# Converting five of sixteen weight pieces inside the first quads, with x ahead of weights in the queue and the last copies ahead of conversions

## The chip, the cores and the metric

One core of a Trainium2 chip. The time is the device time of one execution in microseconds; each kernel was run beside the kernel it is compared with, on the same chip. Fewer microseconds are better.

## The reference, cut to what matters

```python
Y = np.fft.rfft(x, axis=1) * (filt_r + 1j * filt_i)[None]   # x: 8 images, 3008 x 256
x = np.fft.irfft(Y, n=3008, axis=1).astype(np.float32).reshape(24064, 256)
h = x @ w_in                                # w_in: 256 x 2048, float64
g = np.where(h > 0, h, np.exp(np.minimum(h, 0)) - 1)
out = (g @ w_out).astype(np.float32)        # w_out: 2048 x 256, float64
```

The two weights are float64, and the kernel computes in fp32. So the kernel fetches them as pairs of 32-bit words and builds fp32 numbers out of the bits, once, before or beside the first use. That conversion is what the change moves.

## The kernel before

The work of an image is a chain: x is brought in and transformed (`a_first`, `t_first`), multiplied by the filter (`b_unit`, the "products" on VectorE), transformed back (`bi_unit`), written to DRAM as `yd`, read back in another order, and finished by the matmuls `psn` in `n_unit`. Then come "quads": one quad takes one block of positions and a quarter of the hidden width through both weights, each as seven products of a Strassen scheme. TensorE does `phs`, `pha`, `phd` (first weight) and `po` (second weight) in a quad, and ScalarE and VectorE do the copies, the exponential and the combinations between them. There are 192 quads; only the first four to five matter here, because each meets its quarter of the weights for the first time.

A weight piece is 128 x 512 numbers (0.52 MB); there are sixteen, four for each quarter. This is the conversion of one:

```python
def w_split(k):                       # VectorE: mantissa bits and exponent bits
    nc.vector.tensor_scalar(out=m, in0=hi, scalar1=0x000FFFFF, op0=ALU.bitwise_and, ...)
    nc.vector.tensor_scalar(out=e, in0=hi, scalar1=0x7FF00000, op0=ALU.bitwise_and, ...)
def w_float(k):                       # ScalarE: four ACTIVATEs
    nc.scalar.activation(out=l, in_=wds[k][:, :, 0], func=AXT.Identity, scale=2.0 ** -52)
    nc.scalar.activation(out=f, in_=m, func=AXT.Identity, scale=2.0 ** -20, bias=1.0)
    nc.scalar.activation(out=ef, in_=e, func=AXT.Relu, scale=-8.0, bias=edges[:, 0:1])
    nc.scalar.activation(out=e, in_=ef, func=AXT.Relu, scale=-1.0, bias=edges[:, 1:2])
def w_join(k):                        # VectorE: sign, sum, product; for odd pieces four sums
    ...                               # (cut)
    if j % 2 == 1:
        nc.vector.tensor_tensor(out=s1, in0=a21, in1=a22, op=ALU.add)
        ...                           # three more (cut)
```

The order of the program before, with cuts marked. Each engine gets its own instructions in this order:

```python
TICKS = {0: 8, 1: 9, 3: 10, 5: 11, 7: 12, 8: 13, 9: 14}   # step g: piece k
for c in range(NXC):
    x_load_first(c)
    if 0 < c < 5:
        w_fetch(c, nc.sync)           # weights between the pieces of x
...
for c in range(NXC):                  # pieces 0 to 5 while x is transformed
    w_split(c); w_float(c); a_first(c)
    if c > 0:
        w_join(c - 1); w_fetch(c + 4, ...)
nc.sync.dma_start(gs, gs_d)           # the table of the inverse transform
...                                   # pieces 6 and 7 (cut)
for g in range(NG + 2):               # products, inverse transform, yd
    k = TICKS.get(g)
    if k: w_split(k)
    ...                               # bi_unit(g-2), b_unit(g), y_write(g-2), y_read (cut)
    if k: tick(k)                     # w_float(k), w_join(k-1)
w_split(15); tick(15)
w_join(15)
n_unit(0, 0)                          # psn, and after it the quads
```

And the place in a quad at which TensorE waits. `phs` is one accumulation bank; ScalarE copies it out (`keep`) before TensorE may add the next product to it:

```python
def s1(): keep("t1", mm(1, "s", True))                       # phs <- y
def s2(): add("b11", mm(2, "a", True), g["t1"]); done("a")   # pha <- y
def s6(): keep("t2", mm(6, "s", False))                      # phs <- ys: needs the copy of s1
```

## Time and profile before

The median is 2667.32 us (2666.79 to 2667.9, 4 runs). TensorE is busy for 98% of it, so I follow a few marks on TensorE's timeline: where it starts the last x matmuls and the first transpose, where it starts `psn`, where it starts quad 4 (the first matmul with 256 columns), and where it starts a later `psn` that lies well behind everything the change touches.

| mark (us) | before |
|---|---|
| last x matmuls / first transpose | 46.28 / 52.12 |
| first `psn` | 118.17 |
| quad 4 starts | 168.12, that is 49.95 after `psn` |
| later `psn` | 194.85 |

Two rows of TensorE's timeline carry the last two marks of the table. The columns are the start, the busy time, the engine, the line, the operation with output and inputs, and the shapes:

```profile
168.12 1.03 PE L408 MATMUL phs<-y,wi 128*128 128x256 f32 x4
194.85 1.95 PE L360 MATMUL psn<-tn,t 128*128 128x128 f32 x16
```

### The profile page before, as it was taken

Reading aid. Unit: us, or ns where it says so; the run is one execution under the profiler, and the core shown is the slowest. Engines: PE = TensorE matmul, PEld = TensorE weight load, DVE = VectorE, ACT = ScalarE, POOL = GpSimd, SP = SyncE. Lnnn points to the kernel's source line nnn. Section 1 sums busy time; section 2 is a strip of 40 time slices with the busy share of each in tenths; the row PEclk is TensorE's granted clock in tenths of the full one; section 3 lists DMA queues with packets and bytes.
Section 4 is the critical chain, followed back from the end, with each engine's and each line's share of the span. In section 5 each row is a group of like instructions: output and inputs, shape, how many; then the busy total and the mean of one; then the engine's idle time right before and its main releaser. Section 6 shows DMA issues by size and latency. Waiting matters only on the chain.

```text
span 2665.7 us, 37335 instructions
## 1 busy us (share of the span) xinstructions
PE 2601.9 (98%) x13508; PEld 2213.2 (83%) x13508; DVE 1843.9 (69%) x3203; ACT 1507.8 (57%) x2622; POOL 235.6 (9%) x295
## 2 busy tenths in 40 slices
PE   4799999999999999999999999999999999999998
PEld 3388889888898878988889878898789888899887
DVE  4876767767676776767766776676767677666766
ACT  5555555555555555555555555555555555555554
POOL 4000200012000120002100021000210012000000
PEclk7799999999999999999999999999999999999999
DMA  9533411343124231333314242133421233110010
GB/s 277 129 94 92 109 44 38 92 107 94 38 51 123 77 86 38 86 97 80 78 41 102 73 99 74 38 85 96 105 56 38 68 87 87 39 40 19 21 28 17
DMA packets 224712, 202.85 MB, mean 76 GB/s; under 512 B 127586, under 2 KB 191090, under 8 KB 224528
## 3 DMA queue, kind: packets, MB, share of 16 engines
q1 hardware_dynamic: 212064, 167.23, 25.1%
q0 software_dynamic: 11008, 32.52, 4.7%
q8 instruction: 107, 1.75, 0.3%
q10 hardware_dynamic: 1456, 0.72, 0.1%
q14 instruction: 77, 0.63, 0.1%
HBM read 128.52 MB, written 74.97 MB: 76 GB/s over the span
## 4 chain that ended last, share of the span: by engine, by line
PE 95%; DMA 2%; DVE 1%; issue 0%; ACT 0%; SPq 0%; DVEq 0%; ACTq 0%
PE po L490 43%; PE phs L408 25%; PE phd L408 12%; PE pha L408 6%; PE psn L360 3%; PE pva L297 2%; PE psr L297 2%; PE psa L209 2%; DMA f<-in_moe_w_in_dram 1%; DMA xc<-in_x_dram 1%; PE pvb L297 1%; DMA wd<-in_moe_w_out_dram 0%; PE psi L297 0%; PE po L269 0%; DMA t<-yd 0%
## 5 line engine op out<-in xcount | busy, mean ns | idle before, releaser
L490 PE MATMUL po<-g,wo 128*128 128x256 f32 (+1 forms) x5376 | 1296.7, 375 | 0.0
L490 PEld LDWEIGHTS po<-g,wo 128*128 128x128 f32 x5376 | 1015.0, 190 | 129.5 <-issue 16.2
L419 ACT ACTIVATE g<-phs 128x512 f32<-128x512 f32 (+1 forms) x576 | 338.9, 588 | 844.2 <-PE phs L408 843.6
L416 DVE TENSOR_TENSOR g<-phd,g 128x512 f32<-128x512 f32 (+1 forms) x384 | 259.6, 676 | 463.7 <-ACT e L426 278.0
L426 ACT ACTIVATE e<-e 128x512 f32<-128x512 f32 (+1 forms) x768 | 477.3, 621 | 24.4
L408 PE MATMUL phs<-y,wi 128*128 128x256 f32 (+1 forms) x1536 | 395.1, 380 | 0.0
L408 PE MATMUL phs<-ys,wi 128*128 128x256 f32 (+1 forms) x1536 | 387.6, 375 | 2.5 <-ACT g L419 1.5
L430 DVE SCALAR_TENSOR_TENSOR g<-e,g 128x512 f32<-128x512 f32 (+1 forms) x576 | 387.1, 672 | 0.2 <-ACT e L426 0.2
L425 ACT ACTIVATE e<-g 128x512 f32<-128x512 f32 (+1 forms) x576 | 352.9, 613 | 35.4 <-DVE g L416 29.3
L408 PEld LDWEIGHTS phs<-y,wi 128*128 128x128 f32 x1536 | 284.9, 190 | 83.2 <-ACT t L329 34.1
L408 PEld LDWEIGHTS phs<-ys,wi 128*128 128x128 f32 x1536 | 291.4, 190 | 36.4 <-ACT g L419 2.2
L430 DVE SCALAR_TENSOR_TENSOR g<-e,phs 128x512 f32<-128x512 f32 (+1 forms) x192 | 130.0, 677 | 139.2 <-ACT e L426 139.2
L408 PE MATMUL phd<-ys,wi 128*128 128x256 f32 (+1 forms) x768 | 193.9, 375 | 1.8 <-DVE g L416 1.8
L408 PE MATMUL pha<-y,wi 128*128 128x256 f32 (+1 forms) x768 | 193.7, 375 | 0.0
L408 PE MATMUL phd<-y,wi 128*128 128x256 f32 (+1 forms) x768 | 193.7, 375 | 0.0
L425 ACT ACTIVATE e<-phs 128x512 f32<-128x512 f32 (+1 forms) x192 | 112.9, 588 | 141.4 <-PE phs L408 140.6
L318 POOL TENSOR_TENSOR sr<-sr,sp 128x512 f32<-128x512 f32 x56 | 71.1, 1270 | 1256.2 <-DVE sp L311 1256.2
L408 PEld LDWEIGHTS phd<-ys,wi 128*128 128x128 f32 x768 | 145.7, 190 | 18.9 <-DVE g L416 2.5
L408 PEld LDWEIGHTS pha<-y,wi 128*128 128x128 f32 x768 | 145.8, 190 | 16.5
L408 PEld LDWEIGHTS phd<-y,wi 128*128 128x128 f32 x768 | 145.8, 190 | 16.5
L467 DVE TENSOR_TENSOR g<-g,g 128x512 f32<-128x512 f32 (+1 forms) x192 | 130.7, 681 | 6.6
L470 DVE TENSOR_TENSOR g<-g,g 128x512 f32<-128x512 f32 (+1 forms) x192 | 130.7, 681 | 6.7
(134 smaller groups left out, 2393.1 us busy)
## 6 DMA issues: line engine op xcount, KB each, us to landing
yd<-t SPq DMA_DIRECT2D x127, 192.0 KB
t<-yd SPq DMA_DIRECT2D x190, 128.0 KB
z<-t SPq DMA_DIRECT2D x84, 256.0 KB
f<-fd POOLq DMA_DIRECT2D x112, 192.0 KB, 3.6
t<-z SPq DMA_DIRECT2D x224, 96.0 KB
out_dram<-o SPq DMA_DIRECT2D x632, 32.0 KB
tn<-tn_t SPq DMA_DIRECT2D x48, 256.0 KB
xc<-in_x_dram SPq DMA_DIRECT2D x84, 128.0 KB
```

The source lines that it names most:

```text
L297: nc.tensor.matmul(ps[:, u:u + w, :], table[k, v, :], r[k, u:u + w, :], start=n == 0, stop=n == len(rhs) - 1)
L318: nc.gpsimd.tensor_tensor(out=sr, in0=sr, in1=p, op=ALU.add)
L360: nc.tensor.matmul(ps[:, ts(q, P)], t[:, i - 4 * m, ds(dh * P, P)], w[:, i - 4 * m, :], start=True, stop=True)
L408: nc.tensor.matmul(ps[:, a, 0:h], w_in[q][:, COMBO[n], a, :], y[n], start=start and a == 0, stop=True, skip_group_check=True)
L416: nc.vector.tensor_tensor(out=g[o], in0=i0, in1=i1, op=ALU.add)
L419: nc.scalar.activation(out=g[o], in_=i0, func=AXT.Copy)
L425: nc.scalar.activation(out=e, in_=src, func=AXT.Relu, scale=-1.0)
L426: nc.scalar.activation(out=e, in_=e, func=AXT.Exp, scale=-1.0)
L430: nc.vector.scalar_tensor_tensor(out=g[n], in0=es[n], scalar=1.0, in1=src, op0=ALU.subtract, op1=ALU.max)
L467: nc.vector.tensor_tensor(out=b12, in0=b22, in1=b12, op=ALU.subtract)
L470: nc.vector.tensor_tensor(out=g["t4"], in0=g["b21"], in1=g["t2"], op=ALU.subtract)
L490: nc.tensor.matmul(po[i][:, u, 0:h], w_out[q][:, COMBO[n], a, :], g[n][:, a, :], start=q == 0 and a == 0 and n in (1, 3, 6, 4), stop=True, ...
```

## The change

The intent is to shorten what lies ahead of `psn`. Fewer weight pieces stand in the queue ahead of x; fewer are converted while VectorE does the filter's products; no conversion stands on ScalarE between the last product and the last two copies; and pieces 11 to 15, which the first quads do not need at once, are converted inside those quads. The core of the diff (the choice of buffers for the pieces is cut):

```diff
-        m, e, c = wtmp[k % 2]
+        m, e, c = wtmp[k % 2 if k < 10 else 0]
...
-        if j % 2 == 1:
+        if j % 2 == 1 and k < 11:
+            w_sums(k)                      # the four sums, now a function
...
-        TICKS = {0: 8, 1: 9, 3: 10, 5: 11, 7: 12, 8: 13, 9: 14}
+        TICKS = {0: 4, 1: 5, 3: 6, 4: 7, 6: 8}
...
-                if 0 < c < 5:
-                    w_fetch(c, nc.sync)
+                if c in (1, 3):
+                    w_fetch((c + 1) // 2, nc.sync)
...
-                w_split(c)
-                w_float(c)
+                if c % 2 == 0:
+                    w_split(c // 2)
+                    w_float(c // 2)
                 a_first(c)
-                if c > 0:
-                    w_join(c - 1)
-                    w_fetch(c + 4, nc.sync if c < 4 else nc.gpsimd)
+                if c in (2, 4):
+                    w_join(c // 2 - 1)
+                for k in ((), (3,), (4, 5), (6,), (7,), ())[c]:
+                    w_fetch(k, nc.sync)
             nc.sync.dma_start(gs, gs_d)
...
-            w_split(15)
-            tick(15)
-        w_join(15)
+            for k in (9, 10):
+                w_split(k)
+                tick(k)
+                w_fetch(k + 4)
+        w_join(10)
...
         n_unit(0, 0)
+        w_split(11)
+        w_float(11)
...
+        for (quad, place), steps in {
+            (0, 0): ((w_join, 11),),
+            (0, 1): ((w_sums, 11), (w_split, 12), (w_float, 12)),
+            (1, 0): ((w_join, 12), (w_fetch, 15), (w_split, 13), (w_float, 13)),
+            (1, 1): ((w_join, 13),),
+            (2, 0): ((w_sums, 13), (w_split, 14), (w_float, 14)),
+            (2, 1): ((w_join, 14), (w_split, 15), (w_float, 15)),
+            (3, 0): ((w_join, 15),),
+            (3, 1): ((w_sums, 15),),
+        }.items():
```

Place 0 of a quad is its middle, place 1 its end.

More of the change, by code (lines that the diff above doesn't have):

```diff
@@ L547, in w_fetch @@
         q, j = divmod(k, 4)
-        if k in (3, 4):
-            wd = t2p.tile([P, 4, D], FP32, tag="t2", name="wd").rearrange("p u d -> p (u d)")
-        elif k in (10, 11):
+        if k in (10, 11):
             wd = t1p.tile([P, XC, D], FP32, tag="t1", name="wd").rearrange("p u d -> p (u d)")
-        elif k in (6, 7, 8, 9, 15):
+        elif k in (3, 4, 6, 7):
             wd = xp.tile([P, 2, 2, D], FP32, tag="xc", name="wd").rearrange("p k u d -> p (k u d)")
         else:
-            wd = fbufs[{5: 0, 12: 1, 13: 2, 14: 0}.get(k, k)].rearrange("p c u d -> p (c u d)")
+            wd = fbufs[{0: 0, 5: 0, 12: 0, 15: 0, 1: 1, 8: 1, 13: 1}.get(k, 2)].rearrange("p c u d -> p (c u d)")
         wd = wds[k] = wd.bitcast(U32).rearrange("p (a w) -> p a w", w=2)
@@ L606, in w_join, with w_sums @@
                 nc.vector.tensor_tensor(out=dst[:, i], in0=f[:, i], in1=e[:, i], op=ALU.mult)
-        if j % 2 == 1:
-            w = (w_in if j < 2 else w_out)[q]
-            a11, a21, a12, a22, s1, s2, s4 = (w[:, i] for i in range(7))
-            nc.vector.tensor_tensor(out=s1, in0=a21, in1=a22, op=ALU.add)
-            nc.vector.tensor_tensor(out=s2, in0=s1, in1=a11, op=ALU.subtract)
-            nc.vector.tensor_tensor(out=s4, in0=a12, in1=s2, op=ALU.subtract)
-            nc.vector.tensor_tensor(out=a21, in0=a11, in1=a21, op=ALU.subtract)
+        if j % 2 == 1 and k < 11:
+            w_sums(k)
+    def w_sums(k):
+        q, j = divmod(k, 4)
+        w = (w_in if j < 2 else w_out)[q]
+        a11, a21, a12, a22, s1, s2, s4 = (w[:, i] for i in range(7))
+        nc.vector.tensor_tensor(out=s1, in0=a21, in1=a22, op=ALU.add)
+        nc.vector.tensor_tensor(out=s2, in0=s1, in1=a11, op=ALU.subtract)
+        nc.vector.tensor_tensor(out=s4, in0=a12, in1=s2, op=ALU.subtract)
+        nc.vector.tensor_tensor(out=a21, in0=a11, in1=a21, op=ALU.subtract)
     def f_arrange():
@@ L679 @@
                 f_read(0, g, ff[:, g])
-                if g % 2:
-                    w_fetch(NXC + 4 + g // 2)
+                if 3 <= g < 6:
+                    w_fetch((8, 10, 11)[g - 3])
             for g in range(4):
                 t_first(g)
-            for k in (NXC, NXC + 1):
-                w_split(k)
-                tick(k)
-                w_fetch(k + 8)
+            w_split(3)
+            tick(3)
+            w_fetch(9)
             tn_read(0, 0)
@@ L704 @@
                     tick(k)
-            w_split(15)
-            tick(15)
-        w_join(15)
+                    if k == 6:
+                        w_fetch(12)
+            for k in (9, 10):
[3 more added lines that the diff above has]
+        w_join(10)
         for c in range(2):
@@ L722, in at @@
             plan.setdefault((quad, place), []).append((fn, a))
+        for (quad, place), steps in {
[8 more added lines that the diff above has]
+        }.items():
+            for fn, k in steps:
+                at(quad, place, fn, k)
         for c in range(2, XBUFS):
```

## The prediction

> **What bounds the kernel now.** I read the page first, then busy time by stretch, the chain of waits of the first 135 us, the timeline of each engine there, and last the DMA queues in growing windows.
>
> ```profile
> span 2665.7 us, 37335 instructions
> PE 2601.9 (98%) x13508; PEld 2213.2 (83%) x13508; DVE 1843.9 (69%) x3203; ACT 1507.8 (57%) x2622; POOL 235.6 (9%) x295
> ...
> 0.00:100.00 100.00, 61.40 (x329) 38.50 (x332) 59.23 (x116) 55.26 (x101) 33.58 (x65) 0.73 0.80 220
> ...
> 110.00:120.00 10.00, 1.83 (x8) 1.86 (x9) 7.12 (x16) 5.44 (x10) 0.00 (x0) 0.50 0.70 172
> ...
> 140.00:150.00 10.00, 10.00 (x64) 9.72 (x66) 8.26 (x16) 5.49 (x11) 0.00 (x0) 1.00 0.33 85
> ```
>
> In the two stretch rows PE is the first busy figure, PEclk third from the end. Steady state is TensorE at 98%: nothing that the change touches. Only the preparation (to 118.17 us, first matmul psn) and the first four "quads" (to 169 us) can move. Within them:
>
> ```profile
> 46.28 3.76 PE L250 MATMUL psa<-t,x 128*128 128x128 f32 x16 [7.44 <-DMA x<-in_x_dram]
> 64.21 1.08 PE L297 MATMUL pva<-sr,gs 48*64 48x256 f32 x2 [5.02 <-issue]
> 107.53 0.63 ACT L583 ACTIVATE wfl<-wm 128x512 f32<-128x512 uint32 x1 [2.16 <-DVE wm L576]
> 109.43 0.58 ACT L329 ACTIVATE t<-pva 128x512 f32<-128x512 f32 x1
> 110.52 2.98 DMA yd<-t
> 114.06 3.91 DMA t<-yd
> 118.17 3.75 PE L360 MATMUL psn<-tn,t 128*128 128x128 f32 x16 [12.62 <-DMA t<-yd]
> ```
>
> Three limits follow each other: DMA until x's last piece (46.28); VectorE from 55.16 on, where b_unit products and weight conversions queue behind each other without a gap; at the end ScalarE, whose copy at 109.43 stands behind a conversion that itself waited for VectorE, and then write plus read of yd, 7.6 us, untouched by the change. In the quads ScalarE and VectorE have spare time, but TensorE already waits at one place, the second accumulation into phs, until ScalarE has copied phs out:
>
> ```profile
> 133.06 1.02 PE L408 MATMUL phs<-ys,wi 128*128 128x224 f32 x4 [0.90 <-ACT g L419]
> 59.15 0.42 DVE L613 TENSOR_TENSOR wi<-wi 128x256 f32<-128x256 f32 x1
> 60.16 0.68 DVE L593 SCALAR_TENSOR_TENSOR we<-wd,we 128x512 uint32<-128x512 uint32 x1
> 58.19 0.78 ACT L586 ACTIVATE we<-we,edges 128x512 f32<-128x512 uint32 x1
> q1 hardware_dynamic: 3900, 7.85, 61.9%
> q1 hardware_dynamic: 4705, 9.31, 60.4%
> ```
>
> The last two rows are the SyncE queue's MB by 46 and by 56 us.
>
> **What the Trainium skill says.** "ScalarE: Activation LUTs", What ACT_TABLE_LOAD costs: an ACTIVATE takes 186 ns + 0.833 per element with immediates, 93 more with a pointer bias, and neighbours overlap by about 93. For 512 that is 612 and 706 ns; the trace has 0.61 to 0.69 and 0.70 to 0.78, so it agrees. "VectorE: DVE Perf Modes", the TRN2 errata section: (N+151)/0.96, 691 ns for a 512-wide fp32 tensor_tensor; the trace has 0.68 to 0.69. "DMA: Bandwidth & Descriptors", Queues, rings and completion order: completion is not FIFO per issuing engine. The trace agrees: x's last piece has 7.3 MB up to and with it in its queue, and landed when 7.85 MB had moved. "TensorE: Matmul & The Clock Gate", Part 1: after an idle window of about 3.4 us the array runs at half clock until it has been busy for about as long. The trace agrees: PEclk 0.50 in 110 to 120, and psn's 16 matmuls take 3.75 us at 118 against 1.95 at 142.
>
> **The change part by part.** One piece costs (start to start in the timeline) VectorE 0.68 for the split, 2.0 for the join, 1.6 more for the sums of every second piece; ScalarE 2.54 (57.10 to 59.64) for its four ACTIVATEs.
>
> (1) x ahead of weights. Until x's last piece the queue now carries three 0.52 MB weight pieces, not five: about 6.3 MB. Allowing the same 0.5 MB of skew, that is 6.8 MB moved, which was reached near 36 us. So the last x matmuls start near 37, not 46.3; and the copies out of them no longer stand behind piece 5's conversion, which landed only at 49.1. The transposes can begin near 42.5 (before 52.1), the first product on VectorE near 48 (before 62.83); it must also wait for piece 4, 8.0 MB with skew.
>
> (2) But the table gs, needed by the first bi_unit, stays behind the same eight weight pieces: 9.2 MB, near 56 us whatever the order. VectorE will have finished products 0 and 1 and joins up to piece 4 at about 59. So bi_unit 0 starts near 56 (before 64.21), at half clock again, takes 7 us as before, and product 2 starts near 66.3 instead of 74.23: 7.9 us gained.
>
> (3) From product 2 to product 7 VectorE has six products of 2.4, three joins, two sums and three splits: 25.7 us of work; with the TensorE hand-overs I put product 7 at 93 (before 100.96, also 26.7 us after product 2). Then no conversion stands between product 7 and the copies: 2.4 product, 2.1 matmul, 1.2 copies give 98.7, against 110.5 (9.5 us after product 7's start). Another 3.9 gained. psn would start near 106 instead of 118.17: **12 us gained**. Pieces 9 and 10 are converted under the yd round trip, exactly where 14 and 15 were before.
>
> (4) The five late pieces add 5 x 2.54 = 12.7 us to ScalarE and 5 x 2.7 + 3 x 1.6 = 18 us to VectorE, in four quads of about 11.7 us each, in which VectorE is busy about 32 of 46 us. It could nearly fit, were it spread; but queues are in order. In the changed instruction order, pieces 11, 12 and 15 have their ScalarE part in front of the copy of phs that TensorE waits for, and that part waits for a split which stands on VectorE behind the previous quad's last subtraction and, for 12 and 15, behind sums or a join. Times after psn's start, before against after:
> - quad 0: combine and split 11 end near 7.0, conversion 8.7, copy 9.2; TensorE goes on at 9.25 instead of 6.49: 2.8 lost.
> - quad 1: last subtraction 16.6 + 2.8 = 19.3; sums 20.9; split 21.7; conversion (three ACTIVATEs after the split's first half) 23.3; copy 23.8; TensorE at 23.85 instead of 14.89: 9.0 in all, 6.2 more.
> - quad 2: piece 14's split stands behind piece 13's sums, in front of the x sums and the phd addition: about 2 more.
> - quad 3: join 14 and split 15 (2.7) behind the last subtraction, conversion, copy: TensorE at 58.2 instead of 40.4: 6.7 more.
> - quad 4: sums 15 just before use, about 1 more.
> Sum 18.7. The two idle spells of some 7 us bring half clock for about 4 us each, as after 118: up to 4 us more, of which I count 1.5, since the other engines' lags shrink meanwhile. **20 us lost.** TensorE, at 98% afterwards, cannot win it back.
>
> Sum: 2667.5 - 12 + 20 = 2675.5; I shade it to **2674**, since a loss hung on two-engine waits overlaps more often than my addition allows.
>
> **The rivals.** (a) The deferred work hides: VectorE idles 3.5 us before its phd addition in these quads, and ScalarE is busy about 55%. Then only the preparation counts: 2656, or 2650 if gs comes earlier than I think, for VectorE would be ready for product 2 at 60. For it: the totals nearly fit. Against: the order of instructions, and the 0.90 us wait at 133.06, which shows that there is no slack at that copy. (b) The preparation hardly gains: all bytes must still pass, DMA is saturated to 62 us, and gs might slip to 60 because the filter pieces come through POOL's queue sooner. Then the gain is 8 and the time 2680. For it: DMA share above 1.0 to 60 us. Against: the conversions really leave VectorE's busiest stretch. (c) Late weights stall TensorE: pieces 13 and 14 are fetched only when their buffers are free, near psn, and 15 in quad 1. Landing took 6 to 10 us, and they are used 20 us later; I expect nothing, at worst 2685.
>
> **Range and chances.** All cases lie between 2650 and 2690. I give (a) about a quarter of the weight, my sum with its errors nearly all the rest: 2657 to 2686 should hold it 8 times in 10. Two per cent is 53 us; even the preparation without any idle time, or twice the loss, stays inside. Within 2%: 0.98; 0.01 for each side.
>
> **What would show it.** Step 1: last x matmuls near 37 and transposes near 42.5. Step 2: the first pva matmul near 56, waiting for a DMA. Step 3: last pvb copy near 99 and psn near 106, no conversion on ScalarE between. Step 4: TensorE waits on the ScalarE copy of phs of about 3, 7 and 7 us in quads 0, 1 and 3, PEclk below 1 after the latter two; the busy time per stretch equal to before from quad 5 on. It is wrong if quad 4 starts less than 8 us after its old distance of 50 us from psn, or if psn starts before 100 or after 112.

## More of the kernel before

From TensorE's waits between 97 and 215 us (total, times, longest):

```profile
PE psn L360 <- DMA t<-yd: 12.6, 1, 12.6
PE phs L408 <- ACT g L419: 1.5, 2, 0.9
```

The reader sees one long wait, for the trip of `yd` through DRAM, and almost none at the copy of `phs`.

## The result and the profile after

The changed kernel is correct and takes 2681.78 us (median of 4 runs, 2679.35 to 2682.55), against 2667.32 beside it. The ratio is 1.0053 with a 95% interval of 1.0035 to 1.0070: within 2%, but a real loss of about 14 us. Ratios here are the mean time of one kernel's fast runs over the mean of the other's in the same rounds, so they are not quite the ratio of the medians that I quote.

| mark (us) | before | after | difference |
|---|---|---|---|
| last x matmuls end | 50.04 | 40.44 | -9.6 |
| first transpose | 52.12 | 40.28 | -11.8 |
| first product on VectorE | 62.83 | 45.67 | -17.2 |
| first inverse matmul (`pva`) | 64.21 | 56.76 | -7.5 |
| last copy ahead of `yd` ends | 110.5 | 100.1 | -10.4 |
| `psn` | 118.17 | 107.86 | -10.3 |
| quad 4, distance from `psn` | 49.95 | 72.81 | +22.9 |
| later `psn` | 194.85 | 208.44 | +13.6 |

The preparation gained 10.3 us and the first quads lost 23.9 (22.9 by the start of quad 4 and 1.0 inside it). At the last `psn` of the run, 2558.73 before and 2572.32 after, the difference is still 13.59: nothing later moved.

TensorE's timeline in the preparation of the changed kernel shows what still held it:

```profile
33.87 6.57 PE L250 MATMUL psa<-t,x 128*128 128x128 f32 x32 [5.86 <-DMA t<-tf_t]
56.76 1.08 PE L297 MATMUL pva<-sr,gs 48*64 48x256 f32 x2 [9.28 <-DMA gs<-gs_t]
```

In brackets are the idle time before the row and what ended it. x was done early, as intended. After the transposes and the first matmuls on them TensorE stood for 9.28 us until the table `gs` landed, which is behind eight weight pieces in the queue.

TensorE's waits between 97 and 215 us, the same list as before:

```profile
PE phs L408 <- ACT g L419: 17.7, 4, 7.0
PE psn L360 <- ACT wfl L581: 8.9, 1, 8.9
PE po L490 <- DVE wo L614: 0.8, 1, 0.8
```

The wait on the copy of `phs` has grown from 1.5 to 17.7 us. The second line is a wait on the `yd` read that the list puts down to the last thing that ended before it; the ScalarE row that it names has nothing to do with `psn` (in experiments 1 and 3 the list puts the same wait down to `DMA t<-yd`).

The timeline of TensorE in quads 0 to 4 shows the three long waits at this place and what follows them:

```profile
116.83 1.02 PE L408 MATMUL phs<-ys,wi 128*128 128x224 f32 x4 [3.63 <-ACT g L419]
118.49 1.86 PE L408 MATMUL phs<-ys,wi 128*128 128x224 f32 x4 [0.63 <-ACT g L419]
...
132.82 1.86 PE L408 MATMUL phs<-ys,wi 128*128 128x224 f32 x4 [6.96 <-ACT g L419]
134.47 3.19 PE L490 MATMUL po<-g,wo 128*128 128x224 f32 x8
...
169.33 1.86 PE L408 MATMUL phs<-ys,wi 128*128 128x224 f32 x4 [6.49 <-ACT g L419]
170.98 2.57 PE L490 MATMUL po<-g,wo 128*128 128x224 f32 x8
...
180.67 1.03 PE L408 MATMUL phs<-y,wi 128*128 128x256 f32 x4
```

Look at the durations: four `phs` matmuls take 1.86 us after the two longest waits, and after the first wait from the second group on, where they take 1.02 at full clock; eight `po` matmuls take 3.19 and 2.57 instead of 1.68. The stretches of the same time say why (after the stretch and its length, the first figure is the time in which PE was busy; PEclk, the granted TensorE clock with 1.00 for full, is the third from the end):

```profile
118.00:122.00 4.00, 3.51 (x11) 3.24 (x12) 2.80 (x7) 2.02 (x4) 0.00 (x0) 0.57 1.08 199
132.00:139.00 7.00, 6.18 (x20) 5.25 (x24) 4.48 (x8) 1.31 (x3) 1.24 (x2) 0.53 0.24 77
169.00:173.00 4.00, 3.67 (x10) 3.37 (x11) 3.62 (x7) 0.82 (x2) 0.00 (x0) 0.53 0.00 0
```

TensorE is busy, at about half its clock, three times. Why the copy came late in quad 1 is read from ScalarE's timeline and then VectorE's:

```profile
130.34 0.63 ACT L581 ACTIVATE wfl<-wm 128x512 f32<-128x512 uint32 x1 [3.65 <-DVE wm L574]
131.62 0.72 ACT L585 ACTIVATE we<-we,edges 128x512 uint32<-128x512 f32 x1
132.24 0.52 ACT L419 ACTIVATE g<-phs 128x448 f32<-128x448 f32 x1
```

```profile
127.76 0.62 DVE L470 TENSOR_TENSOR g<-g,g 128x448 f32<-128x448 f32 x1
128.30 0.42 DVE L612 TENSOR_TENSOR wo<-wo 128x256 f32<-128x256 f32 x1
129.55 0.42 DVE L615 TENSOR_TENSOR wo<-wo 128x256 f32<-128x256 f32 x1
129.89 0.42 DVE L574 TENSOR_SCALAR wm<-f 128x512 uint32<-128x512 uint32 x1
```

ScalarE was ready at 126.7 for piece 12's second ACTIVATE. It waited 3.65 us for the split, which stands on VectorE behind the previous quad's last subtraction (L470) and four sums of piece 11 (L612 to L615). The copy of `phs`, L419, stands behind the conversion in ScalarE's queue, though its input, four matmuls that started at 123.43, had been ready since about 124.4, and TensorE stands behind the copy.

### The profile page after: what moved, and what is told of

It is laid out like the page before. It is cut to its first block, busy times and chain, and to the rows that moved or that the text cites. A ratio compares the mean times of both kernels' runs of the same rounds, so it can differ in the third digit from the quotient of the medians.

```text
span 2680.3 us, 37330 instructions
## 1 busy us (share of the span) xinstructions
PE 2605.0 (97%) x13508; PEld 2217.6 (83%) x13508; DVE 1842.9 (69%) x3203; ACT 1508.5 (56%) x2622; POOL 235.0 (9%) x295
## 4 chain that ended last, share of the span: by engine, by line
PE 94%; DVE 2%; DMA 2%; ACT 1%; issue 0%; SPq 0%; DVEq 0%; ACTq 0%
PE po L490 42%; PE phs L408 24%; PE phd L408 12%; PE pha L408 6%; PE psn L360 3%; PE pva L297 2%; PE psr L297 2%; PE psa L209 2%; DMA gs<-gs_t 1%; DMA xc<-in_x_dram 0%; DMA x<-in_x_dram 0%; PE pvb L297 0%; DMA tn<-tf_t 0%; DVE g L430 0%; PE psi L297 0%
## 5 line engine op out<-in xcount | busy, mean ns | idle before, releaser
L419 ACT ACTIVATE g<-phs 128x512 f32<-128x512 f32 (+1 forms) x576 | 338.8, 588 | 848.0 <-PE phs L408 847.3
L408 PE MATMUL phs<-ys,wi 128*128 128x256 f32 (+1 forms) x1536 | 390.9, 377 | 17.7 <-ACT g L419 17.7
L470 DVE TENSOR_TENSOR g<-g,g 128x512 f32<-128x512 f32 (+1 forms) x192 | 130.7, 681 | 6.6
```

What stands on the lines that cost most here:

```text
L408: nc.tensor.matmul(ps[:, a, 0:h], w_in[q][:, COMBO[n], a, :], y[n], start=start and a == 0, stop=True, skip_group_check=True)
L419: nc.scalar.activation(out=g[o], in_=i0, func=AXT.Copy)
L470: nc.vector.tensor_tensor(out=g["t4"], in0=g["b21"], in1=g["t2"], op=ALU.subtract)
```

## The experiments

My theory A: the copy of `phs` is held by ScalarE's part of a late conversion, which is held by VectorE's part; the waits and the half clock after them eat the gain. Rivals: B, VectorE's extra work alone is the bound; C, ScalarE's extra work alone is the bound; D, the half clock is a symptom, absorbed by the lags of the other engines. The kernels came in four sets, each with the kernel before on the same chip: its medians were 2667.53, 2666.05, 2666.82 and 2667.05.

### 1. ScalarE's part of the late pieces removed (wrong result)

```diff
         w_split(11)
-        w_float(11)
-            (0, 1): ((w_sums, 11), (w_split, 12), (w_float, 12)),
+            (0, 1): ((w_sums, 11), (w_split, 12)),
             ... the same for 13, 14 and 15
```

> The changed kernel without the ScalarE part (four ACTIVATEs each) of the five late pieces; VectorE's splits, joins and sums stay where they are. The result is wrong on purpose. Theory A (TensorE is held by the ScalarE copy of phs that stands behind a conversion which itself waits for a split on VectorE): the waits of 3.6, 7.0 and 6.5 us at the second phs accumulation in quads 0, 1 and 3 fall to about 1 us each or less, the distance from psn's start to quad 4 falls from 72.8 to 50 to 56 us, and the time from 2681.8 to about 2660 to 2665, below the kernel before. Rival V (VectorE has too much to do in these quads, whatever ScalarE does): the distance stays above 65 us and the time above 2674.

Measured: 2661.49 us, ratio 0.9981 (0.9966 to 0.9996). TensorE's waits in the quads:

```profile
PE phd L408 <- DVE g L416: 5.0, 4, 1.8
PE phs L408 <- ACT g L419: 0.6, 1, 0.6
```

Quad 4 starts 52.45 us after `psn` (161.02 less 108.57): of the 22.9 us lost, 2.5 remain, though VectorE still does all its splits, joins and sums. B falls.

### 2. VectorE's part of the late pieces removed (wrong result)

ScalarE keeps its twenty ACTIVATEs; the late weights are set to zero by GpSimd, so that nothing reads what was never written.

```diff
+    def w_late(k):
+        m, e, c = wtmp[0]
+        wts[k] = m, e, c[:, 0], c[:, 1]
+        w_float(k)
...
-            (0, 0): ((w_join, 11),), ... (3, 1): ((w_sums, 15),),
+            (0, 1): ((w_late, 12),), (1, 0): ((w_fetch, 15), (w_late, 13)),
+            (2, 0): ((w_late, 14),), (2, 1): ((w_late, 15),),
```

> The changed kernel with the ScalarE part of the five late pieces in its place, but without VectorE's splits, joins and sums of them (the late weights are zero, set by GpSimd before the quads; the result is wrong on purpose). Theory A: what remains is one conversion of 2.5 us in front of the copy in quads 0, 1 and 3, with no wait inside it, so the waits of TensorE there are 1 to 3 us instead of 3.6, 7.0 and 6.5, half clock after them mostly goes, the distance psn to quad 4 is 54 to 60 us (72.8 now), and the time 2661 to 2668. Rival S (it is ScalarE's extra 12.7 us of work alone that costs): waits and time stay within 4 us of the changed kernel, above 2677.

Measured: 2668.50 us, ratio 1.0006 (0.9991 to 1.0021), half a microsecond above the range that I had expected.

```profile
PE phs L408 <- ACT g L419: 8.5, 4, 3.3
```

Quad 4 starts 59.06 us after `psn` (169.54 less 110.48), so 9.1 us are lost by ScalarE's work alone. VectorE's part alone costs 2.5, ScalarE's alone 9.1, both together 22.9. The remaining 11.3 us appear only with both parts in place, and the rows above show how one engine's part waits for the other's. Of them 3.3 us are half clock (one restart of 2.9 us here, after a wait of 3.35 us, against 6.2 us in the changed kernel, taken apart below); the rest are waits. That is A, with C as a part of it. (`psn` came 2.6 us later than in the changed kernel, although the order ahead of it is the same. In this execution the first `pva` matmul waited for `gs` until 59.41 instead of 56.76; in the seven profiles with this order it starts between 54.76 and 59.41. I compare distances from `psn` for that reason.)

### 3. All sixteen pieces ahead of the quads

```diff
-            for k in (9, 10):
+            for k in range(9, 16):
                 w_split(k)
                 tick(k)
...
-        w_split(11)
-        w_float(11)
-        for (quad, place), steps in { ... }     # the late plan
```

> The changed kernel with all sixteen pieces converted before the quads: pieces 11 to 15 follow 9 and 10 after the loop, none is left for the quads. The distance of quad 4 from the end of the conversions is as before, and the five pieces cost their VectorE time at the end of the preparation, where it is the only engine with work: 5 x 2.7 + 3 x 1.6 = 18 us, less what fits under the yd round trip (8 us of VectorE idle there). Expected: psn near 108 as in the changed kernel, the combine 8 to 10 us later than in the changed kernel, no wait above 1 us at the phs accumulations of quads 1 and 3, and 2668 to 2675, so below the changed kernel. If late pieces are what makes the change slower, it must be faster than 2681.8; if the early part is to blame, it is as slow or slower.

Measured: 2677.13 us, ratio 1.0041 (1.0027 to 1.0054), correct, a little above what I had expected. `psn` is at 107.93, as in the changed kernel, and then TensorE stands:

```profile
PE phs L408 <- ACT y L362: 15.4, 1, 15.4
```

Seven conversions stand on ScalarE ahead of the copy of `psn`. Quad 4 starts 67.42 us after `psn`. So the loss is not a matter of the quads as such: placed in front of the copy of `psn`, the conversions cost about as much, here 17.5 us, mostly in one wait, instead of 22.9 in several.

### 4. The copies alone, in the kernel before

```diff
-        TICKS = {0: 8, 1: 9, 3: 10, 5: 11, 7: 12, 8: 13, 9: 14}
+        TICKS = {0: 8, 1: 9, 3: 10, 5: 11, 7: 12}
...
-            w_split(15)
-            tick(15)
+            for k in (13, 14, 15):
+                w_split(k)
+                tick(k)
```

> The kernel before with only the end of the preparation changed: pieces 13 and 14 are converted after the loop, together with 15, so the last copies of bi_unit have no conversion in front of them. The last copy then ends near 106.5 to 107.5 us instead of 110.5 and psn starts near 114 to 115 instead of 118.2; but three conversions instead of two (7.6 us) then stand on ScalarE behind the wait for yd, in front of psn's copies, and three joins on VectorE in front of the combine. I expect a net gain of 0 to 2.5 us: 2665 to 2667.5. If the whole 3.5 us came through, 2664 or less.

Measured: 2670.10 us, ratio 1.0024 (1.0008 to 1.0039). I had expected a small gain, and it was a small loss. The last copy does end 4.5 us earlier and `psn` starts at 113.79 instead of 118.17. But TensorE's timeline goes on so:

```profile
113.79 3.75 PE L360 MATMUL psn<-tn,t 128*128 128x128 f32 x16 [8.95 <-ACT wfl L583]
119.19 1.86 PE L408 MATMUL phs<-y,wi 128*128 128x224 f32 x4 [1.64 <-ACT y L362]
...
131.14 1.41 PE L408 MATMUL phd<-ys,wi 128*128 128x224 f32 x4
```

The conversion that no longer stands ahead of the copies stands between `psn` and the copies out of it. TensorE then has several short waits, and the half clock lasts until 132. Quad 4 comes 56.71 us after `psn` instead of 49.95: 4.4 us won, 6.8 lost. The same exchange as in the whole change, at a smaller scale. (The net of 2.4 us lies inside the interval of the timed loss, 2.1 to 10.4 us; the medians differ by 4.0, and one of the four runs took 2676.59.)

### 5. x ahead of weights alone, in the kernel before

```diff
                 x_load_first(c)
-                if 0 < c < 5:
-                    w_fetch(c, nc.sync)
+            for c in range(1, 5):
+                w_fetch(c, nc.sync)
```

> The kernel before with only the order of the queue changed: all six x pieces and their tables ahead of weight pieces 1 to 4. The conversions still stand between x's matmuls and their copies on ScalarE, one piece per step, and piece 5, needed by the last step, has the same bytes in front of it. If that is the limit, the transposes still begin near 52 us and the time is within 2 us of 2667.3. If x's arrival is the limit, the transposes begin near 42 and the time falls by 4 us or more, to below 2663.

Measured: 2665.48 us, ratio 0.9997 (0.9983 to 1.0011): nothing. The last x matmuls start at 43.66 instead of 46.28, but the transposes only at 50.52 instead of 52.12, and the first product is at 62.93, where it was. ScalarE's row shows the reason:

```profile
33.42 0.68 ACT L582 ACTIVATE wfl<-f 128x512 f32<-128x512 uint32 x1 [17.67 <-DMA f<-in_moe_w_in_dram]
```

The conversion of a piece that now lands later stands in ScalarE's queue ahead of the copies of x. Alone, the new queue order does not pay. In the change it comes together with fewer early conversions; these alone were not tried.

### 6. The table `gs` fetched early

```diff
             nc.sync.dma_start(once, once_d)
+            nc.sync.dma_start(gs, gs_d)
...
-            nc.sync.dma_start(gs, gs_d)
```

> The changed kernel with one line moved: the table gs is fetched right after the identity table, ahead of weight pieces 3 to 7. If gs is what the first bi_unit waits for, its first pva matmul starts near 47 to 49 us instead of 56.8 with no wait for a DMA, product 2 on VectorE starts at 57 to 60 instead of 63.9 (then bound by VectorE), psn starts 3 to 6 us earlier (102 to 105 instead of 107.9) and the time is 2676 to 2679. If the gain of the preparation is bound by VectorE or by the filter pieces anyway, psn starts within 1 us of 107.9.

Measured: 2674.26 us, ratio 1.0028 (1.0012 to 1.0045). The first inverse matmul starts at 45.45 without any wait, and `psn` at 98.41, 9.4 us earlier than in the changed kernel; I had expected 102 to 105, and a time of 2676 to 2679. The waits on the copy of `phs` stay (16.0 us), and quad 4 comes 74.04 us after `psn`. So the two halves of the account nearly add: of the 9.4 us gained in the preparation 8.2 are left at the later `psn` (200.22 instead of 208.44), and the quads lose what they lost, 1.2 us more. (The 9.4 us hold more than the wait itself: the first two `pva` matmuls took 0.64 us here, and 1.08 after the wait.)

### 7. The clock: dummy matmuls in the waits, first attempt

To keep TensorE's clock up, dummy matmuls are put into the three waits of quads 0, 1 and 3. They write a free bank that nobody reads; the result is correct.

```diff
+        WARM = {0: 14, 1: 32, 3: 30}
...
+                if n == 3 and i in WARM:
+                    held, ps = bank("warm", (P, 512))
+                    for _ in range(WARM[i]):
+                        nc.tensor.matmul(ps[:, 0:224], w_in[0][:, 0, 0, :], ys[0, 0][1], start=True, stop=True)
+                    banks.insert(0, held)
```

> The changed kernel with idle matmuls (14, 32 and 30 of 128x224, into a free PSUM bank that nobody reads) in front of the waiting phs accumulation in quads 0, 1 and 3, so that TensorE works through most of its wait; results are right. If half clock after the idle spells is a cost on the path, as the doubled matmul times after them suggest (1.5, 2.8 and 1.8 us longer), the matmuls after the spells take their normal 0.92 us per four, PEclk is 1.00 in the stretches from 118 to 180 us, and the time falls by 4 to 6 us, to about 2676 to 2678. If the other engines' lags absorb it, as I assumed for all but 1.5 us in the prediction, the time falls by less than 2 us.

Measured: 2688.12 us, ratio 1.0078 (1.0063 to 1.0093). The run missed its purpose:

```profile
127.22 12.27 PE L790 MATMUL warm<-y,wi 128*128 128x224 f32 x64
```

Thirty-two fp32 matmuls of the program are 64 rows of 0.19 us each, so they lasted 12.27 us where the wait is 6.96, and pushed the real work back.

### 8. The same with half as many, beside the changed kernel again

```diff
-        WARM = {0: 14, 1: 32, 3: 30}
+        WARM = {0: 7, 1: 16, 3: 15}
```

> The changed kernel with dummy matmuls in the three waits on the copy of phs (quads 0, 1 and 3), half as many as in the earlier attempt: 7, 16 and 15 matmuls, which that run's rows (14, 32 and 30 of them took 5.46, 12.27 and 11.51 us) put at about 2.7, 6.1 and 5.8 us, inside the waits of 3.63, 6.96 and 6.49. Correct result. Theory A (the half clock after the stalls lies on the path and was counted at 1.5 where the rows show about 6): the groups after the waits take 0.92 per four instead of 1.86, and the time falls by 3 to 6 us against the changed kernel, to 2676-2679; the second-last marker (later psn) comes near 203-206 instead of 208.6. Rival (the other engines' lags, not TensorE's clock, set the pace after a stall; the half clock is absorbed): groups at full clock, but new waits of the same size and a time less than 2 us below the changed kernel's.

> The changed kernel unaltered, as the reference for the run with the dummies on the same chip. Every theory expects a ratio to the kernel before of 1.0035 to 1.007, as first measured (1.0053), so about 2680 to 2684.

Measured on one chip: 2675.75 us with the dummies, ratio 1.0034 (1.0019 to 1.0049), and 2683.27 for the unaltered changed kernel, ratio 1.0060 (1.0044 to 1.0077). From TensorE's timeline with the dummies:

```profile
124.53 6.22 PE L790 MATMUL warm<-y,wi 128*128 128x224 f32 x32
131.51 1.02 PE L408 MATMUL phs<-ys,wi 128*128 128x224 f32 x4 [0.76 <-ACT g L419]
132.37 1.68 PE L490 MATMUL po<-g,wo 128*128 128x224 f32 x8
...
174.82 1.03 PE L408 MATMUL phs<-y,wi 128*128 128x256 f32 x4
```

The dummies fill the wait, the groups behind it take 1.02 and 1.68 instead of 1.86 and 3.19, and quad 4 starts 66.93 us after `psn` (at 107.89) instead of 72.81. Nothing useful was added or taken away but the clock: 5.9 us, all on the path, as A has it. The time fell by 7.5 us, somewhat more than the 3 to 6 expected; in the second profile of the changed kernel quad 4 lies 73.64 us after `psn`, so the loss itself varies by about 0.8 between executions. D falls for these waits.

### 9. A version that keeps the gain

Two things are drawn from the above: fetch `gs` early, and never put a late conversion, whose split is not yet done, ahead of a copy that TensorE needs. Pieces 9 to 12 are converted under the `yd` trip, whose DMA is issued from SyncE alone, so that ScalarE's queue is free for them. In the changed kernel ScalarE stood there:

```profile
104.15 0.66 ACT L580 ACTIVATE wfl<-f 128x512 f32<-128x512 uint32 x1 [4.04 <-DMA yd<-t]
```

Only 13 to 15 are late, with the split at the end of a quad, the ScalarE part in the middle of the next and the join at its end; and the sums from piece 9 on go to GpSimd.

```diff
+            nc.sync.dma_start(gs, gs_d)          # right after once
-            for k in (9, 10):
+            for k in range(9, 13):
...
-        w_split(11)
-        w_float(11)
+        w_split(13)
...
+            (0, 0): ((w_float, 13),),
+            (0, 1): ((w_join, 13), (w_sums, 13), (w_split, 14)),
+            (1, 0): ((w_float, 14),),
+            (1, 1): ((w_join, 14), (w_split, 15)),
+            (2, 0): ((w_float, 15),),
+            (2, 1): ((w_join, 15), (w_sums, 15)),
```

> A version built from the reasons: gs early; the last write and read of yd on SyncE's queue alone, so that ScalarE isn't blocked and converts pieces 9 to 12 during that round trip; sums of pieces 9, 11, 13 and 15 on GpSimd; only pieces 13 to 15 late, each with its split at the end of one quad, its ScalarE part in the middle of the next (never in front of the phs copy) and its join at that quad's end. If the reasons hold: psn near 102 to 105 us, no wait above 1.5 us at the phs accumulations, quad 4 at 50 to 54 us from psn, and 2651 to 2658, below both kernels. If the late work costs by its amount wherever it stands, quad 4 is above 58 us from psn and the time above 2660.

Measured: correct, 2657.66 us (5 runs), ratio 0.9968 (0.9956 to 0.9981). It beats both kernels, the one before by about 8.5 us and the changed one, by the two ratios, by about 23. `psn` is at 97.38 and quad 4 comes 60.92 us after it: the preparation gains 20.8, the quads still lose 11.0. The time is as expected, but its parts are not: I had put `psn` at 102 to 105, waits on the copy of `phs` at 1.5 us at most (the longest is 2.27) and quad 4 at 50 to 54 us after `psn`; a distance above 58 was to be a sign that late work costs by its amount wherever it stands. For the 11.0 us that is not excluded. TensorE's timeline shows where they lie: 5.7 by the first `po` of quad 0, with PEclk 0.50 from 97 to 112; 1.4 in the wait of 2.27 us in quad 1 and 1.7 in the half clock after it; the rest in quads 2 and 3. Which of the moved parts cause them was not tested. The sums on GpSimd have a price that I had not counted. While one ran, VectorE's addition of a join took 1.21 us instead of 0.68. That fits the Trainium skill, "SBUF — State Buffer", section "SBUF: two separate sides": a VectorE instruction with two SBUF inputs and a GpSimd instruction that reads SBUF take turns at a shared pair of ports under an exclusive lock, and the loser is blocked.

### 10. Dummies ahead of `psn`

`psn` itself runs at half clock in all these kernels. The same dummies (256 columns) were put into the wait for the `yd` read, 13 in the version of 9 and 24 in the kernel before.

```diff
+        held, ps = bank("warm", (P, 512))
+        for _ in range(13):                      # 24 in the kernel before
+            nc.tensor.matmul(ps[:, 0:256], w_in[0][:, 0, 0, :], w_in[0][:, 1].rearrange("p a b -> p (a b)"), start=True, stop=True)
+        banks.insert(0, held)
         n_unit(0, 0)
```

> The best version so far (2657.66, ratio 0.9968) with 13 dummy matmuls of 256 columns (estimate 5.6 us at full clock, about 7.5 when the first part runs at half) ahead of the first forward product psn, inside its wait of 8.33 us on the yd read. Theory A (the half clock is a cost on the path wherever TensorE restarts): psn takes 1.95 instead of 3.75, the groups after it 0.92 instead of 1.86, and the time falls by 2 to 5 us, to 2653-2656, ratio 0.995 to 0.996. Rival (other engines set the pace): time within 1 us of 2657.7, the waits after psn (1.08, 1.46, 0.63) growing by what the matmuls save.

> The kernel before with 24 such dummy matmuls (estimate 10.3 us at full clock) inside its 12.62 us wait ahead of psn. Theory A: psn takes 1.95 instead of 3.75 and the next group 0.92 instead of 1.27, so about 2 us off, to 2664-2666, ratio 0.9990 to 0.9995. Rival: no change beyond 0.5 us.

Measured: 2657.82 us, ratio 0.9969 (0.9957 to 0.9982), and 2667.19 us, ratio 1.0007 (0.9993 to 1.0020). No gain, but not a test of A either, because the dummies did not hold the clock. In the kernel before:

```profile
107.08 10.63 PE L716 MATMUL warm<-wi 128*128 128x256 f32 x48
119.90 3.65 PE L360 MATMUL psn<-tn,t 128*128 128x128 f32 x16 [2.20 <-DMA t<-yd]
```

They ran at full clock and ended 2.20 us ahead of `psn`, and `psn` still took 3.65 us, where 1.95 is its time at full clock. In the version of 9 the idle time left was 3.15 us, `psn` took 3.01, and quad 4 came 59.13 us after it instead of 60.92; but `psn` itself was 0.9 us later, so the later `psn` was only 0.9 us earlier (184.15 against 185.03), too little for the timed runs to show. What the half clock of `psn` costs stays open. Why `psn` itself came 0.9 and 1.7 us later than without the dummies is not known either.

## Why the prediction was right, and where its sum was off

The time was inside the range, and its class, within 2%, is right. The middle, 2674, was 7.8 us low. The mechanism is the one predicted, and each step can be placed beside its number.

**Step 1**, right and on the early side: the last two groups of x matmuls run from 33.87 to 40.44 without a break, so the last one starts near 37, as predicted; transposes at 40.28 for 42.5, first product at 45.67 for 48.

**Step 2**, the wait right, product 2 not: the first `pva` matmul came at 56.76 for 56, waiting for the DMA of `gs`, and experiment 6 shows by removal that this wait held `psn` back. But product 2 came at 63.93, not at 66.3. I had carried over the old distance of 10.0 us from the first `pva` to product 2. In the kernel before, VectorE worked without a gap until 74.0 and held product 2 at 74.23; in the changed kernel it had been idle for 7.08 us, and the distance was 7.2. The wait for `gs` is not the only one in force, either: in the second profile of the changed kernel `gs` came 2.0 us earlier (`pva` at 54.76), product 3 then waited 4.50 us for TensorE, and `psn` was still at 108.24. Rival (b) put the gain at 8 because `gs` might slip to 60. It did not, and the gain of 10.3 lies between its 8 and my 12.

**Step 3**, the mechanism right, the size a little off. That product 7 came at 92.63 for 93 is luck. From product 2 on it took 28.7 us and not 26.7, which made up for the 2.4 us of step 2. The 25.7 us of VectorE work count six products, but only five lie between the starts of products 2 and 7, and product 7 is added once more afterwards. The work was 23.5 us, and 5.2 us of waits on TensorE came to it (1.39 and 3.79), where about 1 us was allowed for. From product 7 on, the last copy ended at 100.1 for 98.7 and `psn` came at 107.86 for 106. The gain was 10.3 us and not 12. The term that failed is the 2.1 us put down for the inverse matmuls that are left after product 7. Product 7 ended at 95.10 and these matmuls at 98.95: 3.85 us, where it was 2.1 before (103.45 to 105.55). The whole group, which overlaps the product, took 4.9 us from 94.05, and 3.15 before (from 102.40). The clock granted in that stretch, 90 to 100 us, was 0.71, against 0.94 in the ten us of the kernel before (100 to 110) that hold the same group.

**Step 4**, the waits right, the clock after them mis-sized. From the distances to `psn` on TensorE's timeline I take the loss apart, row against row of before:

| term | predicted | measured |
|---|---|---|
| quad 0, wait on the copy | 2.8 | 2.5 (8.97 against 6.49) |
| quad 1, wait on the copy | 6.2 | 6.1 |
| quad 2, piece 14 ahead of the phd addition | 2 | 1.4 |
| quad 3, wait on the copy | 6.7 | 6.8 |
| quad 4, sums of piece 15 | 1 | 1.0 |
| half clock after the waits | 1.5 | 6.2 (1.5, 2.9 and 1.8) |
| sum | 20 (20.2 before rounding) | 23.9 |

The measured terms are differences of restart times, so they add up. Experiment 8 gives the half clock a second time and independently: 5.9 us. With the dummies the restarts lie 8.99, 23.62 and 57.28 us after `psn`; I had predicted 9.25, 23.85 and 58.2 for the waits alone. So the chain from the previous quad's last subtraction over sums, split, conversion and copy to TensorE was right to within 1 us, and experiments 1 and 2 show that it needs both engines.

What failed here is one term: "up to 4 us more, of which I count 1.5, since the other engines' lags shrink meanwhile". There were three idle spells that brought half clock, not two: the wait of 3.63 us in quad 0, with 0.63 us more one group later, was enough. And the lags did not absorb it. The Trainium skill had the pattern, in "TensorE: Matmul & The Clock Gate", section "HAM oscillation — how this bites in real kernels": each wait that is long enough costs its own cold restart. The trace agrees, with 1.5, 2.9 and 1.8 us lost in three restarts. A wait on the bound engine should be counted with its restart.

The sum then closes. I had -12 + 18.7 + 1.5 and took off 1.5 for overlap; measured are -10.3 + 17.7 + 6.2, and 1.0 after the last `psn`: the profiled spans differ by 14.6, the last `psn` by 13.6. The discount for overlap had no ground: the waits cost 17.7 of the 18.7 us that the addition allowed. The 1.0 at the end was not looked into; the stretch from the later `psn` to the end of the span is 2470.9 us in the kernel before and 2471.4 to 2471.9 in four profiles of the changed kernel and near kin of it.

**Rival (a)**, that the deferred work hides, was given a quarter of the weight and falls. Totals nearly fitted, and with ScalarE's part or VectorE's part taken out alone most of the loss went; but queues in order do not let totals decide. **Rival (c)**, late weights, did not occur: no wait on a weight's DMA stands in TensorE's list.

## What to carry to other kernels

When work is moved off the preparation into a steady loop, do not compare totals of busy time: find, for each engine, the first instruction behind the moved work that the bound engine waits for, and ask what that work itself waits for. Work that crosses two engines (split on one, convert on the other, join on the first) belongs at places where its input is already done and no copy is due behind it. And count a long wait on TensorE with a restart at half clock. Here every wait of 3.35 us or more on the copy of `phs` brought one, at 1.5 to 2.9 us where it was taken apart; of the shorter ones some did (2.27 us in experiment 9) and some did not (2.67 us in experiment 2).

## What the Trainium skill lacked or had wrong

- "TensorE: Matmul & The Clock Gate", Part 1, puts the drop to half clock after an idle window of about 3.4 us. Here shorter idle times sufficed: after 10.63 us of dense matmuls at full clock and 2.20 us without any, `psn` took 3.65 us instead of 1.95 (PEclk 0.99 from 118 to 120 us, 0.58 from 120 to 124). Idle times of 0.76 to 1.13 us (experiment 8) did not bring it. Between them these runs show no length at which it begins: 2.27 us in experiment 9 brought it, 2.67 us in experiment 2 did not.
- The same page says that the array is warm after about 3.4 us of sustained work, and speaks of short idle times between groups of matmuls ("A second HAM failure mode") without giving a length. In experiment 4, with waits of 1.64, 1.49 and 0.63 us among the matmuls, half clock lasted from 113.8 to about 132 us.
- "FP8 and Floating Point Precision", TensorE Precision Notes, says that a true fp32 matmul takes four passes. No run here shows the passes one by one. What the trace shows for one matmul of 224 columns is two matmul rows of 0.19 us each (32 matmuls in the program, 64 rows in the trace); no place there says so, and it cost me experiment 7.
- "DMA: Bandwidth & Descriptors", Issuing engines are not separate DMA queues, treats the choice of issuing engine as a matter of issue time. The page also says that a DMA's semaphore wait happens on the issuing sequencer, but not what this costs the engine. Here a DMA issued from ScalarE had to wait in that engine's queue for the write before it, and ScalarE's next ACTIVATE began 4.04 us after the one before had ended.
